# Cached attention with a gated linear unit, one core: keys and probabilities transposed by VectorE in 32x32 blocks instead of by TensorE

## The chip, the core and the metric

The kernel runs on one core of one Trainium2 chip. A core has five engines that run their own instruction streams and wait for each other by semaphores: TensorE (matrix products; PE in the profile, PEld for its weight loads), VectorE (DVE), ScalarE (ACT), GpSimd (POOL) and SyncE (SP), which here only issues transfers. Data lies in HBM, in SBUF (128 partitions) and in PSUM, where TensorE writes its products. Sixteen DMA engines move data between HBM and SBUF. The metric is the device time of one execution in microseconds (us).

## The reference

What is computed, cut to its core (all arrays bf16):

```python
xn = layernorm(x)                                # x: [8, 1, 512]
q = (xn @ wq)                                    # 32 heads of 128
k = k_cache[:, :, 8192 - 2048:, :]               # 8 batches x 8 key heads, last 2048 rows
v = v_cache[:, :, 8192 - 2048:, :]               # each key head serves 4 query heads
scores = einsum("bhqd,bhkd->bhqk", q, k) * 128 ** -0.5
o = einsum("bhqk,bhkd->bhqd", softmax(scores), v)
s = o.reshape(8, 1, 4096) @ wo
g = (sigmoid(xn @ w_gate) * (xn @ w_up)) @ w_down   # inner width 1792
out = x + s * silu(g)
```

The window of both caches is 8 x 8 x 2048 x 128 numbers each, 33.6 MB, and the weights are 14 MB.

## The kernel before

**Slots and transfers.** Nine SBUF slots of 2 MB (`slots`) hold weights and tiles of the caches. A list `todo`, filled at lines 171 to 192, fixes the order of all transfers: w_gate, w_up, w_down with some small side loads, wq, then K and V tiles, with V three tiles behind K, then wo in four pieces. `pump` issues the next transfer on SyncE's queue as soon as a slot is empty, and `free` gives a slot back at the place in the program where its last reader stands. The side loads (`want_side`, line 122) carry the 384 rows of w_down that the 128-partition load `want_down` leaves out; each touches 3, 5 or 9 partitions.

**A cache tile** (`want_cache`) holds half of the key heads of one batch: four heads `l`, 32 partitions `p` each, with partition 4p + l, and 64 rows `c` of 128 numbers in each partition. So one batch has two K tiles and two V tiles, i = 0 and 1.

**The head of the program** normalises x, computes the gated unit (L278, L294, L366), the queries (`q_ps`, L352: 32 matmuls, four at a time on four column strips of the array), turns them by TensorE (L380) and lays them into `qm_sb`, where each head's four columns stand in a band of zeros, so that a shifted view puts them into any group of four rows.

**The batch loop** (from line 647) is an order of work written out by hand. Each batch has 16 steps. Each step transposes 8 blocks of a K tile on TensorE (`k_transposes`, L456), which VectorE copies from PSUM to `kT_sb` (L461); tasks hang on the steps:

- `scores` (L474): every second step, four matmuls of 512 columns side by side on four strips of 32 columns. A row of `s_ps` is one query head and one of four parts j of its keys.
- `row_max` (L487, L494): the maximum of each of the 128 rows, then four exponentials, each over 32 rows x 512, into `p_buf`.
- `stat_rows`, `factor`, `spread` (L506 to L556): the four parts of a head have maxima of their own; these steps bring them together and make one factor for each row, on one partition.
- `p_transposes` (L563, L568): 16 transposes of the probabilities by TensorE, copied by VectorE to `pT_sb`. Their operand is read in steps of 32 bytes.
- `value` (L584): the products with V, two batches later. Up to batch 4 these are pairs of matmuls of 512 columns on two strips, from batch 5 on fours of 256 columns on four strips.
- `combine`, `normalise`, `turn` (L604, L614, L623, L632, L639): scale the output, pick the right blocks, and lay them as a column into `oP_sb`.

A K slot is freed behind its last transposes, a V slot behind its last value matmul. Behind the loop follow the last two batches' rest, and the product with wo (L706, 128 matmuls of 128 columns), the gate and the residual (L717, L719) and four small output transfers (L721).

Of the kernel before, what the change touches and what calls it, by code (L numbers as in the profile page):

```python
# [10 lines left out]
def kernel(  # L11
# [24 lines left out]
    G = 4  # L36
# [5 lines left out]
    CH = CU // 2  # L42
    NU = NQ * NJ
    NR = NU * rep
# [19 lines left out]
        tc.tile_pool(name="ps_t", bufs=4, space=bass.MemoryType.PSUM)  # L64
# [5 lines left out]
        tc.tile_pool(name="ps_o", bufs=1, space=bass.MemoryType.PSUM)  # L70
# [40 lines left out]
    LOW, SF = (5, 5, 3, 3), 15  # L111
    MID, SM = 9, 4
    SP = 4 * max(LOW)
    M_AT = 32
    MP = 4 * MID
    MT = 11
    m0 = MT * P
    m1 = m0 + SF * sum(LOW)
    assert m1 + SM * MP == F
    side = {}  # L120

    def want_side(w, q, at, count, rows, base, of):
        def f(tag=None):
            if tag:
                t = slots.tile([P, SF, w.shape[1]], bf16, name="side", tag=tag)
                nc.gpsimd.memzero(t[:M_AT])  # L126
                side["t"] = t
                rows_of[("side", 0)] = (t, tag)
                for r in range(SF):
                    weights[("wd_sb", MT + r)] = t[: M_AT + MP if r < SM else SP, r]  # L130
            q0.dma_start(  # L131
                out=side["t"][at + q : at + q + 4 * (count - 1) + 1 : 4, :rows].rearrange(
                    "p s n -> p (s n)"
                ),
                in_=w[base : base + of * count * rows, :].rearrange(
                    "(p q s) n -> q p (s n)", q=of, s=rows
                )[q % of],
            )

        todo.append((not side, f))  # L140
        side["asked"] = True
# [32 lines left out]
    sides = []  # L174
    for q in range(4):
        sides.append((q, 0, LOW[q], SF, m0 + q // 2 * 2 * LOW[0] * SF, 2))
        sides.append((q, M_AT, MID, SM, m1, 4))
# [13 lines left out]
    for t0, t1 in ((0, 16), (16, 26), (26, 30), (30, RT)):  # L191
# [13 lines left out]
    perm = consts.tile([P, P], bf16, name="perm")  # L205
    nc.gpsimd.tensor_copy(  # L206
        out=perm[:].rearrange("k (l p) -> k l p", l=G),
        in_=ident[:].rearrange("k (p l) -> k l p", l=G),
    )


    x_f = work.tile([B, D], f32, name="x_f")
    nc.vector.tensor_copy(out=x_f[:], in_=x_bf[:])
    stats = work.tile([B, nc.vector.BN_STATS_DIM], f32, name="stats")
    nc.vector.bn_stats(out=stats[:], in_=x_f[:])
# [7 lines left out]
    xn_bf = work.tile([B, D], bf16, name="xn_bf")  # L223
    nc.vector.tensor_scalar(  # L224
        out=xn_bf[:],
        in0=x_f[:],
# [7 lines left out]
    for kt in range(KT):  # L234
        nc.tensor.transpose(  # L235
            out=xnT_ps[:, kt, :],
            in_=xn_bf[:].rearrange("b (p kt) -> b kt p", kt=KT)[:, kt, :],
            identity=ident[:B, :B],
        )
    xnT_sb = work.tile([P, KT, Z], bf16, name="xnT_sb")  # L240
    nc.vector.memzero(xnT_sb[:])
    nc.vector.tensor_copy(out=xnT_sb[:, :, :B], in_=xnT_ps[:])  # L242
# [5 lines left out]
    h_side = work.tile([B, SF, M_AT + MP], bf16, name="h_side")  # L248
# [4 lines left out]
    M0 = Z - rep  # L253
    qm_sb = work.tile([P, B, Hkv, M0 + Z], bf16, name="qm_sb")
    nc.gpsimd.memzero(qm_sb[:])
    p_buf = [work.tile([P, PG, G, CU], bf16, name=f"p_buf{i}") for i in range(2)]
    for t in p_buf:
        nc.gpsimd.memzero(t[:])
# [16 lines left out]
    for k in range(F // FC):  # L275
        g_ps = ps_t.tile([B, FC], f32, name="g_ps", tag="t")
        for kt in range(KT):
            nc.tensor.matmul(  # L278
                g_ps[:],
                lhsT=xnT_sb[:, kt, :B],  # L280
# [9 lines left out]
    h_bf = ktpool.tile([P, CU * P], bf16, name="h_bf", tag="kT")  # L290
    for k in range(F // FC):
        u_ps = ps_t.tile([B, FC], f32, name="u_ps", tag="t")
        for kt in range(KT):
            nc.tensor.matmul(  # L294
                u_ps[:],
                lhsT=xnT_sb[:, kt, :B],
# [12 lines left out]
    for h in range(2):  # L309
# [10 lines left out]
    nc.gpsimd.tensor_copy(  # L320
        out=h_side[:, :SM, M_AT:],
        in_=h_bf[:B, m1:F].rearrange("b (p t) -> b t p", t=SM),
    )
    cuts = [h_bf[:B, :m0].rearrange("b (p t) -> b t p", t=MT)[:, t] for t in range(MT)]
    rows = [P] * MT + [M_AT + MP] * SM + [SP] * (SF - SM)
    cuts += [h_side[:, t, : rows[MT + t]] for t in range(SF)]
# [5 lines left out]
    for k, t0, t1 in ((M_AT + MP, MT, MT + SM), (SP, MT + SM, MT + SF)):  # L332
        nc.scalar.copy(out=hT_sb[:k, t0:t1, :B], in_=hT_ps[:k, t0:t1])
# [13 lines left out]
    q_ps = [ps_t.tile([P, D], f32, name="q_ps", tag="t") for _ in range(2)]  # L347
    for kt in range(KT):
        for e in range(2):
            for g in range(G):  # L350
                c0 = (G * e + g) * D
                nc.tensor.matmul(  # L352
                    q_ps[e][Z * g : Z * (g + 1), :],
                    lhsT=xnT_sb[:, kt, :],
                    rhs=weights[("wq_sb", kt)][:, c0 : c0 + D],
                    start=(kt == 0),
                    stop=(kt == KT - 1),
                    tile_position=(0, Z * g),
                    skip_group_check=True,
# [15 lines left out]
    for e in range(2):  # L375
        q_bf = ktpool.tile([P, D], bf16, name="q_bf", tag="kT")
        nc.scalar.mul(out=q_bf[:], in_=q_ps[e][:], mul=scale)
        qT_ps = ps_t.tile([P, rep, G, Z], bf16, name="qT_ps", tag="t")
        for r in range(rep):
            nc.tensor.transpose(  # L380
                out=qT_ps[:, r].rearrange("p g z -> p (g z)"),
                in_=q_bf[:, r * Dh : (r + 1) * Dh],
                identity=ident[:],
            )
        nc.vector.tensor_copy(  # L385
            out=qm_sb[:, :, G * e : G * (e + 1), M0 : M0 + rep].rearrange(
                "p b g r -> p r g b"
            ),
            in_=qT_ps[:, :, :, :B],
        )  # L390
# [13 lines left out]
    for j in range(NB):  # L404
# [12 lines left out]
    Hh = G * rep  # L417
    turn_rows = consts.tile([P, P], bf16, name="turn_rows")
    nc.gpsimd.tensor_copy(
        out=turn_rows[:].rearrange("k (x l r) -> k x l r", x=NU, l=G),  # L420
        in_=ident[:].rearrange("k (l x r) -> k x l r", x=NU, l=G),
    )
    sel_e = consts.tile([P, 2, Hq], f32, name="sel_e")
    for e in range(2):
        nc.vector.reduce_sum(
            out=sel_e[:, e, :].rearrange("k (i h) -> k i h", i=NQ),
            in_=ident_f[:].rearrange(
                "k (i m e h) -> k e i h m", i=NQ, m=NJ // 2, e=2
            )[:, e],
            axis=AX.X,  # L430
        )

    o_ps = ps_o.tile([P, NJ, Dh], f32, name="o_ps")
    sel_j = ident_f[:].rearrange("k (i j h) -> k j i h", i=NQ, j=NJ)
    m_ps = ps_m.tile([P, 512], f32, name="m_ps", tag="m")
    top_ps = m_ps[0:1, 0:P]
    sum_ps = m_ps[0:1, P : 2 * P]
    fac_ps = m_ps[:, 2 * P : 2 * P + 1]
# [3 lines left out]
    kT = {}  # L442
    s_ps = {}
    pT = {}
    st = {}
    row = {}
    fac = {}

    def k_transposes(b, u, h):
        i, j = u // NJ, u % NJ  # L450
        k_sb = k_tiles[(b, i)][0]
        if h == 0:
            kT[(b, u)] = ktpool.tile([P, CU, P], bf16, name="kT_sb", tag="kT")
        kT_ps = ps_t.tile([P, CH, P], bf16, name="kT_ps", tag="t")
        for c in range(CH):
            nc.tensor.transpose(  # L456
                out=kT_ps[:, c, :],
                in_=k_sb[:, j * CU + h * CH + c, :],
                identity=perm[:],
            )  # L460
        nc.vector.tensor_copy(  # L461
            out=kT[(b, u)][:, h * CH : (h + 1) * CH, :], in_=kT_ps[:]
        )
        if j == NJ - 1 and h == 1:
            free(k_tiles.pop((b, i)))

    def scores(b, u):
        i, j = u // NJ, u % NJ
        if u == 0:
# [285 lines left out]
```

## Time and profile before

| What | Value |
|---|---|
| median of 3 runs | 199.12 us (199.09 to 199.34) |
| the profiled execution | 199.33 us, of which the span from first to last instruction is 197.5 us |
| TensorE busy | 157.4 us (80%), 2112 matmuls |
| TensorE weight loads | 103.1 us (52%) |
| VectorE busy | 125.4 us (63%), 245 instructions |
| ScalarE busy | 40.7 us (21%) |
| GpSimd busy | 11.0 us (6%) |
| moved by DMA | 81.32 MB, mean 412 GB/s |
| clock granted to TensorE | mean 0.965 of full speed |

The page of the profile has six parts: busy time of each engine; the span in 40 equal slices, with a digit for the busy tenths of each engine, of the DMA engines, and of the clock granted to TensorE; the DMA queues; the chain of work that ended last; the costliest groups of instructions by source line; and the transfers. A group's line reads: source line, engine, operation, output and inputs, shape, count, then busy us and mean ns of one, then the idle time of the engine just before them and what ended it. Matmuls are pipelined: the 389 ns of a score matmul run from its start to its last result, while the next group may start sooner. The timeline lists start (us) and length (us) of instructions in order of time.

### The profile page before, as it was taken

The numbers are of one execution on the slowest core, as the hardware profiler recorded it, in microseconds if no ns is written. First come the engines' busy times: TensorE is split into PE (matmuls) and PEld (weight loads), VectorE is DVE, ScalarE is ACT, GpSimd is POOL, SyncE is SP. The second block draws the span as 40 slices with busy tenths as digits, with TensorE's granted clock in tenths as the row PEclk, the third lists the DMA queues.
The fourth block names the chain that finished last, engine by engine and source line by source line (L and its number), as shares of the span: only waits on it lengthen the run. The fifth ranks groups of instructions, "written<-read, shape, count | busy, mean of one in ns | idle before, by whom it ended". The sixth has DMA issues, their size and how long they took to land.

```text
span 197.5 us, 4796 instructions
## 1 busy us (share of the span) xinstructions
PE 157.4 (80%) x2112; PEld 103.1 (52%) x2112; DVE 125.4 (63%) x245; ACT 40.7 (21%) x95; POOL 11.0 (6%) x22
## 2 busy tenths in 40 slices
PE   0089559999788898799979987999799979976733
PEld 0034325776664565466545654566466556655531
DVE  4623106999797696679666965796669658935201
ACT  0522022006306001600160016001600160071000
POOL 8910200000000000000000000000000000000000
PEclk9999859999999999999999999999999999999975
DMA  6999999999999999999999999999999999999980
GB/s 205 424 440 435 431 434 435 425 425 431 423 425 425 438 428 435 431 425 428 422 433 431 435 425 433 428 418 428 428 438 431 428 428 431 428 423 425 428 366 21
DMA packets 6396, 81.32 MB, mean 412 GB/s; under 512 B 812, under 2 KB 820, under 8 KB 1624
## 3 DMA queue, kind: packets, MB, share of 16 engines
q1 hardware_dynamic: 6328, 81.01, 96.6%
q8 instruction: 16, 0.26, 0.5%
q10 hardware_dynamic: 48, 0.01, 0.0%
q14 instruction: 4, 0.03, 0.0%
HBM read 81.01 MB, written 0.01 MB: 410 GB/s over the span
## 4 chain that ended last, share of the span: by engine, by line
DMA 73%; PE 22%; POOL 3%; SPq 0%; issue 0%; DVE 0%; POOLq 0%
DMA v_sb<-in_A_v_cache_dram 46%; DMA wo_sb<-in_A_wo_dram 14%; PE kT_ps L456 11%; DMA wq_sb<-in_A_wq_dram 7%; DMA k_sb<-in_A_k_cache_dram 6%; PE o_ps L584 4%; PE s_ps L474 3%; POOL side L126 2%; PE m_ps L614 1%; PE fin_ps L706 1%; PE pT_ps L563 1%; SPq L131 0%; POOL perm L206 0%; POOL hT_sb L245 0%; DVE prod L717 0%
## 5 line engine op out<-in xcount | busy, mean ns | idle before, releaser
L461 DVE COPY kT_sb<-kT_ps 128x1024 bf16<-128x1024 bf16 x128 | 84.2, 683 | 28.9 <-PE kT_ps L456 25.0
L456 PE MATMUL kT_ps<-perm,k_sb 128*128 128x128 bf16 x1024 | 72.6, 220 | 3.7 <-DMA k_sb<-in_A_k_cache_dram 3.7
L456 PEld LDWEIGHTS <-k_sb 128*128 128x128 bf16 x1024 | 58.8, 98 | 26.1 <-issue 16.8
L584 PE MATMUL o_ps<-v_sb,pT_sb 128*32 128x256 bf16 (+1 forms) x352 | 36.5, 327 | 9.0 <-DMA v_sb<-in_A_v_cache_dram 7.6
L474 PE MATMUL s_ps<-kT_sb,qm_sb 128*32 128x512 bf16 x256 | 25.6, 389 | 1.3 <-DVE kT_sb L461 1.1
L494 ACT ACTIVATE p_buf<-s_ps,st 32x512 bf16<-32x512 f32 x32 | 21.7, 679 | 15.4 <-DVE st L487 15.1
L584 PEld LDWEIGHTS <-pT_sb 128*32 128x32 bf16 (+1 forms) x352 | 12.3, 101 | 21.7 <-issue 19.7
L604 ACT ACTIVATE o_sb<-o_ps,fac 128x512 f32<-128x512 f32 (+1 forms) x8 | 4.9, 608 | 60.9 <-PE o_ps L584 60.9
L568 DVE COPY pT_sb<-pT_ps 128x1024 bf16<-128x1024 bf16 x16 | 10.8, 676 | 1.8 <-PE pT_ps L563 1.8
L474 PEld LDWEIGHTS <-qm_sb 128*32 128x32 bf16 x256 | 7.0, 93 | 8.0 <-issue 1.3
L563 PE MATMUL pT_ps<-turn_rows,p_buf 128*128 128x128 bf16 x128 | 10.7, 227 | 0.0
L563 PEld LDWEIGHTS <-p_buf 128*128 128x128 bf16 x128 | 9.4, 149 | 0.2 <-issue 0.2
L521 ACT ACTIVATE w_row<-w 1x128 f32<-1x128 f32 x8 | 2.5, 309 | 30.6 <-DVE w L514 30.6
L235 PE MATMUL xnT_ps<-ident,xn_bf 8*128 8x8 bf16 x4 | 0.3, 176 | 10.6 <-DVE xn_bf L224 10.6
L385 DVE COPY qm_sb<-qT_ps 128x128 bf16<-128x128 bf16 x2 | 1.4, 881 | 8.7 <-PE qT_ps L380 8.7
L301 DVE TENSOR_TENSOR h_bf<-sig,u_ps 8x448 bf16<-8x448 f32 x4 | 2.4, 608 | 6.6 <-PE u_ps L294 6.1
L278 PE MATMUL g_ps<-wg_sb,xnT_sb 128*8 128x448 bf16 x16 | 5.7, 544 | 0.3 <-DVE xnT_sb L242 0.3
L494 ACT ACTIVATION_READ_ACCUMULATOR p_buf<-s_ps,st 32x1 f32 x32 | 5.9, 184 | 0.0
L706 PE MATMUL fin_ps<-wo_sb,oP_sb 128*32 128x128 bf16 x128 | 3.3, 263 | 3.1 <-DMA wo_sb<-in_A_wo_dram 3.1
L487 DVE TENSOR_REDUCE st<-s_ps 128x1 f32<-128x512 f32 x8 | 5.4, 681 | 0.5 <-PE s_ps L474 0.5
L235 PEld LDWEIGHTS <-xn_bf 8*128 8x128 bf16 x4 | 0.2, 117 | 10.6 <-DVE xn_bf L224 10.6
L352 PE MATMUL q_ps<-wq_sb,xnT_sb 128*32 128x512 bf16 x32 | 3.1, 526 | 3.2 <-DMA wq_sb<-in_A_wq_dram 3.2
(88 smaller groups left out, 92.0 us busy)
## 6 DMA issues: line engine op xcount, KB each, us to landing
k_sb<-in_A_k_cache_dram SPq DMA_DIRECT2D x16, 2048.0 KB
v_sb<-in_A_v_cache_dram SPq DMA_DIRECT2D x16, 2048.0 KB
wq_sb<-in_A_wq_dram SPq DMA_DIRECT2D x2, 2048.0 KB
wo_sb<-in_A_wo_dram SPq DMA_DIRECT2D x1, 2048.0 KB
wg_sb<-in_B_w_gate_dram SPq DMA_DIRECT2D x2, 896.0 KB
wu_sb<-in_B_w_up_dram SPq DMA_DIRECT2D x2, 896.0 KB
wd_sb<-in_B_w_down_dram SPq DMA_DIRECT2D x1, 1408.0 KB
wo_sb<-in_A_wo_dram SPq DMA_DIRECT2D x1, 1280.0 KB
```

Of the source, the lines that this page charges most:

```text
L126: nc.gpsimd.memzero(t[:M_AT])
L278: nc.tensor.matmul(g_ps[:], lhsT=xnT_sb[:, kt, :B], rhs=weights[("wg_sb", kt)][:, k * FC : (k + 1) * FC], start=(kt == 0), stop=(kt == KT ...
L456: nc.tensor.transpose(out=kT_ps[:, c, :], in_=k_sb[:, j * CU + h * CH + c, :], identity=perm[:],)
L461: nc.vector.tensor_copy(out=kT[(b, u)][:, h * CH : (h + 1) * CH, :], in_=kT_ps[:])
L474: nc.tensor.matmul(s_ps[b][NR * l : NR * (l + 1), :], lhsT=qm_sb[:, b, i * G + l, o : o + Z], rhs=t[:, :, PG * l : PG * (l + 1)], start=(u ...
L487: nc.vector.tensor_reduce(out=st[b][:], in_=s_ps[b][:], axis=AX.X, op=ALU.max, negate=True)
L494: nc.scalar.activation(out=p_buf[b % 2][rows, :, l, :], in_=s[rows, :].rearrange("k (c p) -> k p c", p=PG), func=AF.Exp, bias=st[b][rows, ...
L563: nc.tensor.transpose(out=pT_ps[:, c, :], in_=p_buf[b % 2][:, :, :, h * CH + c].rearrange("k p l -> k (p l)"), identity=turn_rows[:],)
L568: nc.vector.tensor_copy(out=pT[b][:, h * CH : (h + 1) * CH, :], in_=pT_ps[:])
L584: nc.tensor.matmul(o_ps[r] if b < WIDE else o_ps[r, 0:2], lhsT=pT[b][:, c, r], rhs=x, start=(c == 0), stop=(c == CU - 1), tile_position=(0 ...
L604: nc.scalar.activation(out=o[:, :n], in_=o_ps[:, :n], func=AF.Copy, scale=fac.pop(b)[:])
L706: nc.tensor.matmul(fin_ps[Z * j : Z * (j + 1), :], lhsT=oP_sb[:, t, :], rhs=weights[("wo_sb", t)][:, j * P : (j + 1) * P], start=(t == 0), ...
```

## The change

The keys are no longer transposed by TensorE. `k_turn` takes a quarter of a K tile, reads each pair of bf16 numbers as one 4-byte number, and has VectorE transpose all 32x32 blocks of these in place; no PSUM and no copy are involved. After that a partition holds one pair of the 128 numbers, for the keys of one group of 32 partitions (a group `a` holds eight p of all four heads). So `scores` multiplies with a stationary operand of full width, `q_wide`, in which the query stands once for each of the four groups of partitions, in blocks, with zeros around; two halves j of the pairs, four heads l and two members e of the pair make 16 matmuls of 512 columns for a tile, and the moving operand takes every eighth number (16 bytes apart). A row of `s_ps` is now (group a, tile i, head l, query r), a column (c, h).

One maximum per query head replaces the maxima of four parts: `row_max` reduces the rows and turns the 128 values into one row; `head_max` takes the maximum over the four groups and brings it back to all rows by a matmul with one column. `exps` then makes four exponentials over all 128 rows, one for each l, with a scale of 1 or 0 and a bias of minus the maximum or -1000, so that rows of another head give 0. `p_turn` transposes the probabilities as pairs in 32x32 blocks by VectorE. `factor` adds up the sums by one matmul.

`widen` copies the queries of a batch into one of two `q_wide` buffers on GpSimd, four copies per batch; a batch has eight steps instead of 16. The query matmuls use the full array. K slots are freed behind the scores. The values are pairs of matmuls on two strips in all batches, four rows c at a time, and have two PSUM buffers. The side loads carry 128 rows of w_down (8 rows per partition, in two halves each), and the 128-partition load 13 rows per partition instead of 11. The first 16 of 32 products with wo are done as 16 matmuls of 512 columns, copied by ScalarE and folded in by fp32 matmuls (`fold`).

The diff, cut to its core:

```diff
-    LOW, SF = (5, 5, 3, 3), 15
-    MID, SM = 9, 4
+    LOW, SF, SH = (5, 5, 3, 3), 8, 4
     SP = 4 * max(LOW)
-    M_AT = 32
-    MP = 4 * MID
-    MT = 11
+    MT = 13
     m0 = MT * P
...
-                    q_ps[e][Z * g : Z * (g + 1), :],
-                    lhsT=xnT_sb[:, kt, :],
...
+                    q_ps[i][:],
+                    lhsT=xnT_sb[:, kt, X0 - B * l : X0 - B * l + P],
...
+        nc.vector.transpose(
+            out=qT[:, i].rearrange("p r j z e -> p (r j z e)").bitcast(f32),
+            in_=q_bf[:].bitcast(f32),
+        )
+
+    def widen(b):
+        t = q_wide[b % 2]
+        for a in range(PG // B):
+            g = slice(Z * a, Z * (a + 1))
+            nc.gpsimd.tensor_copy(
+                out=t[g, : NW * P].rearrange(
+                    "p (i x e c) -> p i x e c", i=NQ, x=2 * G, e=2
+                )[:, :, :, :, M0 + Z * a : M0 + Z * a + rep],
+                in_=qT[g].rearrange("p i r j (l b) e -> p i (j l) b e r", b=B)[
+                    :, :, :, b
+                ],
+            )
 
...
-        kT_ps = ps_t.tile([P, CH, P], bf16, name="kT_ps", tag="t")
-        for c in range(CH):
-            nc.tensor.transpose(
-                out=kT_ps[:, c, :],
-                in_=k_sb[:, j * CU + h * CH + c, :],
-                identity=perm[:],
-            )
-        nc.vector.tensor_copy(
-            out=kT[(b, u)][:, h * CH : (h + 1) * CH, :], in_=kT_ps[:]
-        )
...
+    def k_turn(b, s):
+        i, j = s // NJ, s % NJ
+        x = (
+            k_tiles[(b, i)][0][:, j * CU : (j + 1) * CU, :]
+            .rearrange("p c d -> p (c d)")
+            .bitcast(f32)
+        )
+        nc.vector.transpose(out=x, in_=x)
+
+    def scores(b, i):
+        if i == 0:
+            s_ps[b] = ps_s.tile([P, CT, 2 * NA], f32, name="s_ps", tag="s")
+        k = k_tiles[(b, i)][0][:].rearrange(
+            "p c (j h l e) -> p j l e c h", j=2, h=2 * NA, l=G
+        )
+        for n in range(NW // NQ):
+            j, l, e = n // (2 * G), n // 2 % G, n % 2
+            o = (i * (NW // NQ) + n) * P + M0 - NL * i - rep * l
             nc.tensor.matmul(
-                s_ps[b][NR * l : NR * (l + 1), :],
-                lhsT=qm_sb[:, b, i * G + l, o : o + Z],
-                rhs=t[:, :, PG * l : PG * (l + 1)],
-                start=(u == 0),
-                stop=(u == NU - 1),
-                tile_position=(0, NR * l),
-                skip_group_check=True,
-            )
-
+                s_ps[b][:],
+                lhsT=q_wide[b % 2][:, o : o + P],
+                rhs=k[:, j, l, e],
+                start=(i == 0 and n == 0),
+                stop=(i == NQ - 1 and n == NW // NQ - 1),
+            )
+        free(k_tiles.pop((b, i)))
 
...
+        nc.tensor.transpose(out=top_ps, in_=st.pop(b)[:], identity=ident_f[:])
+
+    def head_max(b):
+        low = small.tile([1, NA, NQ * NL], f32, name="low")
+        nc.vector.tensor_reduce(
...
+        nc.tensor.matmul(
+            all_ps,
+            lhsT=low[:].rearrange("o a x -> o (a x)"),
...
+        bias = small.tile([P, G], f32, name="bias")
+        nc.vector.scalar_tensor_tensor(
+            out=bias[:],
+            in0=mask[:],
+            scalar=all_ps,
+            in1=away[:],
+            op0=ALU.mult,
+            op1=ALU.add,
+        )
+        row[b] = bias
+
+    def exps(b):
+        bias = row.pop(b)
         s = s_ps.pop(b)
+        p_buf[b] = ppool.tile([P, CT // 2, 2 * NA, G, 2], bf16, name="p_buf")
+        sums[b] = small.tile([P, G], f32, name="sums")
         for l in range(G):
-            rows = slice(NR * l, NR * (l + 1))
             nc.scalar.activation(
-                out=p_buf[b % 2][rows, :, l, :],
-                in_=s[rows, :].rearrange("k (c p) -> k p c", p=PG),
+                out=p_buf[b][:, :, :, l, :],
+                in_=s[:].rearrange("k (c e) h -> k c h e", e=2),
                 func=AF.Exp,
-                bias=st[b][rows, :],
-                accum_out=sums[rows, :],
-            )
...
+                bias=bias[:, l : l + 1],
+                scale=mask[:, l : l + 1],
+                accum_out=sums[b][:, l : l + 1],
+            )
+
+    def p_turn(b):
+        pT[b] = ppool.tile([P, NQ, CT // 2, NL, 2], bf16, name="pT_sb")
+        nc.vector.transpose(
+            out=pT[b][:]
+            .rearrange("p i c x e -> p (i c x e)")
+            .bitcast(f32)
+            .rearrange("p (i c x) -> p c i x", i=NQ, x=NL),
+            in_=p_buf.pop(b)[:].rearrange("k c p l e -> k (c p l e)").bitcast(f32),
+        )
 
...
+        nc.tensor.matmul(
+            sum_ps,
+            lhsT=spread_f[:].rearrange("k i m x e -> k (i m x e)"),
+            rhs=sums.pop(b)[:],
+            start=True,
+            stop=True,
         )
         fac[b] = small.tile([P, 1], f32, name="fac")
-        nc.vector.tensor_copy(out=fac[b][:], in_=fac_ps)
-
...
+        nc.vector.reduce_sum(out=fac[b][:], in_=sum_ps, axis=AX.X)
+        nc.vector.reciprocal(out=fac[b][:], in_=fac[b][:])
+
...
+    NS = NQ * NJ
     for b in range(B):
...
+        tasks = {s: [] for s in range(NS)}
         if b >= 1:
+            tasks[0].append(lambda: scores(b - 1, 1))
+            tasks[1].append(lambda: row_max(b - 1))
+            tasks[2].append(lambda: head_max(b - 1))
+            tasks[2].append(lambda: exps(b - 1))
+            tasks[6].append(lambda: p_turn(b - 1))
+            tasks[6].append(lambda: factor(b - 1))
+        tasks[0].append(lambda: widen(b))
+        tasks[4].append(lambda: scores(b, 0))
+        if b >= 2:
+            for s in range(NJ, NS):
+                n = (s - NJ) * NN // NJ
+                tasks[s].append(lambda n=n: values(b - 2, n, n + NN // NJ))
         if b >= 3:
...
+            tasks[0].append(lambda: combine(b - 3))
+            tasks[3].append(lambda: normalise(b - 3))
+            tasks[5].append(lambda: turn(b - 3))
+        for s in range(NS):
+            k_turn(b, s)
             for f in tasks[s]:
                 f()
 
...
+    RG = 16
+    f_ps = ps_t.tile([P, D], f32, name="f_ps", tag="t")
+    for t in range(RG):
+        g = slice(Z * (t % G), Z * (t % G + 1))
+        nc.tensor.matmul(
+            f_ps[g, :],
+            lhsT=oP_sb[:, t, :],
+            rhs=weights[("wo_sb", t)],
+            start=(t < G),
+            stop=(t >= RG - G),
+            tile_position=(0, g.start),
+            skip_group_check=True,
+        )
+    f_sb = ktpool.tile([P, D], f32, name="f_sb", tag="kT")
+    nc.scalar.copy(out=f_sb[:], in_=f_ps[:])
+    for t in range(RG, RT):
+        if t == 26:
+            fold(fin_ps, f_sb, False, False)
```

## The prediction

> **What bounds the kernel now.** I read the 40 slices first, then the queues, then the chain that ended last, then the groups, and last the timeline and the windows of the end.
>
> ```profile
> DMA  6999999999999999999999999999999999999980
> ...
> q1 hardware_dynamic: 6328, 81.01, 96.6%
> q8 instruction: 16, 0.26, 0.5%
> ...
> DMA 73%; PE 22%; POOL 3%; SPq 0%; issue 0%; DVE 0%; POOLq 0%
> ```
>
> The DMA engines are full from the first slice to the last but one. Queue q1 takes 96.6% of 197.5 us on 16 engines, 190.8 us of each, and its packets run from 1.8 to 193.4 us: no gap is left. q8 fetches instructions, 16 packets of 16 KB at 929 ns (the packets of the trace), 0.93 us of each engine. The 22% of TensorE in the chain are stretches in which the transfers ran on anyway. So the time is a start of 1.8 us, 191.6 us of full DMA engines, and a tail of 4.1 us behind the last packet. The changed kernel moves the same cache and weights; it is faster only through fewer fetches or a shorter tail, and slower only if computation falls so far behind that the transfers wait for slots, or that the last batch ends after the last weights are there.
>
> How much room there is: a 2 MB tile takes 4.9 us (k15 ends 162.95 us, k14 153.20, with one V tile between them), a batch of two K and two V tiles 19.6 us. Issues of cache tiles lie 18 us or more ahead of their first packets from the second batch on.
>
> ```profile
> L461 DVE COPY kT_sb<-kT_ps 128x1024 bf16<-128x1024 bf16 x128 | 84.2, 683 | 28.9 <-PE kT_ps L456 25.0
> L456 PE MATMUL kT_ps<-perm,k_sb 128*128 128x128 bf16 x1024 | 72.6, 220 | 3.7 <-DMA k_sb<-in_A_k_cache_dram 3.7
> L456 PEld LDWEIGHTS <-k_sb 128*128 128x128 bf16 x1024 | 58.8, 98 | 26.1 <-issue 16.8
> L474 PE MATMUL s_ps<-kT_sb,qm_sb 128*32 128x512 bf16 x256 | 25.6, 389 | 1.3 <-DVE kT_sb L461 1.1
> L563 PEld LDWEIGHTS <-p_buf 128*128 128x128 bf16 x128 | 9.4, 149 | 0.2 <-issue 0.2
> L487 DVE TENSOR_REDUCE st<-s_ps 128x1 f32<-128x512 f32 x8 | 5.4, 681 | 0.5 <-PE s_ps L474 0.5
> ```
>
> These are the groups that the change replaces (L456, L461, L563) or prices.
>
> **Part 1: instructions removed.** 1,024 transposes of keys and 128 of probabilities go, with their weight loads. The built program has 1,474 rows on TensorE, 4,091 before, so 16 fetches become about 5.8: 10 × 0.929 / 16 = 0.6 us less per engine if spread evenly. The side loads of w_down shrink with it (384 rows to 128; the other 256 join the 128-partition load), same bytes. Even so engines may end unevenly: the last packets ended between 192.6 and 193.4 us. I take **-0.6** (0 to -0.9).
>
> **Part 2: turning the keys.** 64 transposes of 128x1024 pairs and 8 of probabilities replace 144 copies of 0.68 us. The trace has no VectorE transpose. Nearest below is the copy, 683 ns. A reduction of 512 elements took 681 ns, one of 128 (L264) 274 ns: 1.06 ns an element, so 1024 at one per cycle take 0.274 + 0.95 = 1.22 us. The upper end is L267, which reads the same 128 elements in steps of 64 bytes, in 356 ns: at its 2.1 ns an element, 2.1 us. Each block reads whole runs, so I take 1.22. VectorE then has 9 × 1.22 + 2 × 0.68 + about 1.0 = 13.3 us in 19.6: not a bound. At 2.1 us it would have 21.3, 1.7 × 8 = 14 us too much.
>
> [...]
>
> **Part 3: scores.** 32 matmuls of 512 columns a batch, as before, but over the full array, not four side by side. Alone one streams at 213 ns: pairs of 512-column o_ps matmuls follow each other in 0.21 to 0.24 us in the trace, and fours of 256 columns in 0.10 to 0.11. So 0.33 us for four becomes 0.85. New is the moving operand: its columns lie 16 bytes apart. No matmul of before does that. From below: 213 ns. The nearest row on the same engine are weight loads:
>
> ```profile
> 166.26 0.45 PEld L456 LDWEIGHTS <-k_sb 128*128 128x128 bf16 x8 [0.21 <-issue]
> 166.67 0.58 PEld L563 LDWEIGHTS <-p_buf 128*128 128x128 bf16 x8
> ```
>
> Columns of k_sb lie side by side, those of p_buf 32 bytes apart. Start to start the median is 56 and 63 ns: 63 / 128 × 512 = 252 ns. From above: VectorE's L267 against L264 pays 0.64 ns an element more, 213 + 328 = 541 ns. I take 250 ns, since it is the engine's own read path, and 213 to 541 for the range.
>
> [...]
>
> **Part 4: the order, which is now a chain.** On both engines each step waits for the one in front, once per batch, counted from the last turn of one batch to that of the next: scores of the second half 16 × 0.25 + 0.2 (389 ns from start to end, less 213) = 4.2; row maximum 0.68; a turn 1.22 (it covers the transpose of the maxima); the maximum per head, 512 elements read, 0.68; matmul and bias 0.4; a turn 1.22; scores of the first half 4.0; eight pairs of value matmuls at 0.213, 1.7; turn(b-3) and its copy 0.5; a turn, the probabilities and the last turn 3.66; the factor 0.3. Sum **18.6 us**, 17.4 with 213 ns, against 19.6 us of data. The exponentials (4 × 0.86 on ScalarE, as now) fit beside it. A K slot comes free after its scores, some 10.5 us behind its landing; before it was 7.4 (k15 there at 164.5, its slot used by SP at 171.9): 3 us out of 18 of lead. So the chain stays under the transfers by 1.0 to 2.2 us a batch and I charge nothing; cover gone, each microsecond over counts 7 times.
>
> The head: 32 query matmuls of the full array, 6.8 us against 3.1, and POOL's four copies per batch (0.3 to 0.45 us like L312) put the first turn at about 35.5 us instead of 33.2. The first slot so freed carries a load whose first packet is at 74 us. Nothing.
>
> **Part 5: the tail.**
>
> ```profile
> 188.81 1.08 PE L706 MATMUL fin_ps<-wo_sb,oP_sb 128*32 128x128 bf16 x64 [1.12 <-DMA wo_sb<-in_A_wo_dram]
> ...
> 191.86 2.28 PE L706 MATMUL fin_ps<-wo_sb,oP_sb 128*32 128x128 bf16 x64 [1.97 <-DMA wo_sb<-in_A_wo_dram]
> ```
>
> The first 64 become 16 wide ones and a ScalarE copy (0.6), done by 191. Into the 2.28 us behind 191.86 come four fp32 folds, eight rows; the like at L337 took 0.43 us at full clock, so up to 0.86 at the half clock here, less the 0.39 us that TensorE idles there between landings: 0.04 to 0.47. I take **+0.2**.
>
> **Sum.** -0.6 + 0.2 = -0.4: span 197.5 to 197.1, the profiled execution 199.33 to 198.9, and, as that one stands 0.2 over the median, **198.7 us** on 199.12. Its own range is 197.9 to 199.4.
>
> **Rivals.**
>
> *The clock is halved and the chain overshoots (slower).* The place is the 4.2 us between the two halves of the scores, where TensorE has only the small matmuls of the maxima and of normalise, about 1.1 us.
>
> ```profile
> 183.44:186.85 3.41, 2.55 (x39) 2.10 (x38) 0.46 (x2) 0.47 (x1) 0.00 (x0) 1.00 0.98 422
> 186.85:190.27 3.42, 1.53 (x68) 1.27 (x68) 0.59 (x2) 0.00 (x0) 0.00 (x0) 1.00 0.95 402
> 190.27:193.70 3.43, 1.84 (x56) 1.48 (x56) 0.00 (x0) 0.00 (x0) 0.00 (x0) 0.50 0.60 240
> ```
>
> Columns: busy time of PE, PEld, DVE, ACT, POOL, the clock, DMA. After a window with TensorE busy 75% the clock stayed 1.00, after 45% it was 0.50; windows of 57% elsewhere kept it. A half-clock window of 3.41 us costs 1.7 us of a burst. One a batch: 17.4 + 1.7 = 19.1, still hidden, or at 250 ns 20.3, 0.7 × 7 = 5 us. Two: 22, 17 us. So 200 to 216, about 204; it decides from 1.0 to 2.2 us of loss a batch. For it: the gap is in the order of the code; against: one lost window is absorbed at 213 ns. [...]
>
> *Strided scores at half rate or worse (slower).* At 430 to 541 ns the chain grows by 32 × 0.18 to 0.29: 24.4 to 27.9 us, 4.8 to 8.3 over, seven times: 232 to 257.
>
> *Nothing gained.* The fetches lie on engines that are not last, the fold costs 0.5: 199.0 to 199.4.
>
> **Chances.** Forecast 0.45 (a part of it gains under 0.2%, about what a measurement of this kernel can tell from no change), nothing gained 0.2, half clock 0.22, strided scores or slow turns 0.13. Faster by over 0.2% 0.42, within 0.2% 0.23, slower 0.35. The range 197.9 to 209 takes in the first three but the rival's far end.
>
> **What would show it.** L465 at 1.2 us; the new scores spaced 0.21 to 0.25 us; clock 1.00 from 30 to 190 us; SP waiting, yet DMA nines in every slice; five to six packets on q8; the last o_sb before 188 us. Wrong if 0.50 stands in the middle windows, if scores lie 0.4 us apart, or if DMA slices fall under nine.

## The result, and the profile after

The changed kernel takes **374.16 us** (median of 4 runs, 372.93 to 375.95), the kernel before 199.13 beside it: 1.879 times as long (95% interval 1.871 to 1.888). The prediction was 198.7 us with a range to 209. Here and below medians hold all runs of a kernel, ratios leave disturbed ones out.

The page of the changed kernel, the slices, the two queues and the chain by engine and by line:

```profile
PEclk9999555555555855565555655565555655585698
DMA  8999999945141954169505762277505960320000
...
q1 hardware_dynamic: 6288, 81.01, 53.3%
q8 instruction: 6, 0.10, 0.1%
...
PE 81%; DVE 8%; DMA 6%; issue 2%; POOL 1%; SPq 0%; ACT 0%; ACTq 0%; DVEq 0%
PE s_ps L476 59%; PE o_ps L568 14%; DMA wq_sb<-in_A_wq_dram 4%; DVE k_sb L465 3%; PE m_ps L596 3%; DMA wu_sb<-in_B_w_up_dram 3%; DVE st L487 1%; PE m_ps L506 1%; DVE low L497 1%; PE q_ps L337 1%; POOL q_wide L371 1%; PE m_ps L550 1%; DVE pT_sb L541 1%; DVE oP_sb L621 1%; PE f_ps L679 0%
```

The same 81.01 MB move, but from the ninth slice on the DMA digits fall: transfers wait for slots. 81% of the chain is TensorE now, and most of that is one line, the scores. The groups and, from the timeline of TensorE, the scores of one half:

```profile
L476 PE MATMUL s_ps<-k_sb,q_wide 128*128 128x512 bf16 x256 | 222.5, 1036 | 11.9 <-POOL q_wide L371 6.0
L465 DVE STREAM_TRANSPOSE k_sb<-k_sb 128x1024 f32<-128x1024 f32 x64 | 75.5, 1218 | 0.0
...
L568 PE MATMUL o_ps<-v_sb,pT_sb 128*64 128x512 bf16 x256 | 53.5, 560 | 0.6 <-DVE fac L558 0.6
```

```profile
161.92 3.62 PE L568 MATMUL o_ps<-v_sb,pT_sb 128*64 128x512 bf16 x16
165.48 13.91 PE L476 MATMUL s_ps<-k_sb,q_wide 128*128 128x512 bf16 x16
```

Sixteen scores take 13.9 us: start to start they lie 838 to 861 ns apart in the trace, where I had taken 250. They do so at both clocks: 20 such distances stand in stretches with a granted clock of 1.00, 213 in stretches of 0.50. The o_ps pairs do follow the clock, 213 to 216 ns a pair at 1.00 and 426 at 0.50. So a score's time does not follow TensorE's clock; whether the step of its operand sets its time is what experiments 1 and 2 test. And the clock is halved though TensorE is busy all through these stretches (windows: busy PE, PEld, DVE, ACT, POOL, clock, DMA share, GB/s):

```profile
149.30:152.70 3.40, 3.40 (x5) 0.48 (x4) 0.00 (x0) 0.00 (x0) 0.00 (x0) 0.50 0.00 0
152.70:156.10 3.40, 3.40 (x5) 0.49 (x4) 0.00 (x0) 0.00 (x0) 0.00 (x0) 0.50 0.00 0
```

**Where the 176.7 us between the spans (197.45 and 374.15) lie.** The row maximum (L487) stands once in each batch. In before the first starts at 45.4 us, the last at 173.6; in after at 66.4 and 343.5. So 21.0 us come up to the first, 148.9 in the seven batches between (41.1 us each in the middle, 19.5 before), and 6.8 behind the last. By spacing: 256 scores × (0.86 − 0.213) = 166 us. Values at half clock come to it, up to 128 pairs × 0.214 = 27 us, and what the transfers would have taken anyway goes off; how these two divide is not worked out here.

### The profile page after: what moved, and what is told of

It reads as the page before. It is cut to its first block, busy times and chain, and to the rows that moved or that the text cites. A ratio compares the mean times of both kernels' runs of the same rounds, so it can differ in the third digit from the quotient of the medians.

```text
span 374.1 us, 2156 instructions
## 1 busy us (share of the span) xinstructions
PE 321.6 (86%) x833; PEld 81.7 (22%) x834; DVE 113.3 (30%) x151; ACT 40.5 (11%) x87; POOL 21.3 (6%) x53
## 3 DMA queue, kind: packets, MB, share of 16 engines
q1 hardware_dynamic: 6288, 81.01, 53.3%
HBM read 81.01 MB, written 0.01 MB: 217 GB/s over the span
## 4 chain that ended last, share of the span: by engine, by line
PE 81%; DVE 8%; DMA 6%; issue 2%; POOL 1%; SPq 0%; ACT 0%; ACTq 0%; DVEq 0%
PE s_ps L476 59%; PE o_ps L568 14%; DMA wq_sb<-in_A_wq_dram 4%; DVE k_sb L465 3%; PE m_ps L596 3%; DMA wu_sb<-in_B_w_up_dram 3%; DVE st L487 1%; PE m_ps L506 1%; DVE low L497 1%; PE q_ps L337 1%; POOL q_wide L371 1%; PE m_ps L550 1%; DVE pT_sb L541 1%; DVE oP_sb L621 1%; PE f_ps L679 0%
## 5 line engine op out<-in xcount | busy, mean ns | idle before, releaser
L476 PE MATMUL s_ps<-k_sb,q_wide 128*128 128x512 bf16 x256 | 222.5, 1036 | 11.9 <-POOL q_wide L371 6.0
L465 DVE STREAM_TRANSPOSE k_sb<-k_sb 128x1024 f32<-128x1024 f32 x64 | 75.5, 1218 | 0.0
L476 PEld LDWEIGHTS <-q_wide 128*128 128x128 bf16 x256 | 31.2, 126 | 182.2 <-issue 176.0
L568 PE MATMUL o_ps<-v_sb,pT_sb 128*64 128x512 bf16 x256 | 53.5, 560 | 0.6 <-DVE fac L558 0.6
L530 ACT ACTIVATE p_buf<-s_ps,bias,mask 128x512 bf16<-128x512 f32 x32 | 25.1, 805 | 167.1 <-DVE bias L514 167.1
L487 DVE TENSOR_REDUCE st<-s_ps 128x1 f32<-128x512 f32 x8 | 5.5, 691 | 107.7 <-PE s_ps L476 107.7
L568 PEld LDWEIGHTS <-pT_sb 128*64 128x64 bf16 x256 | 19.8, 152 | 33.2 <-issue 28.3
L371 POOL COPY q_wide<-qT 32x128 bf16<-32x128 bf16 x32 | 12.8, 400 | 216.4 <-PE s_ps L476 214.9
L596 PE MATMUL m_ps<-ident_f,o_sb 128*128 128x32 f32 x56 | 12.4, 383 | 2.5 <-DVE bias L514 2.5
L596 PEld LDWEIGHTS m_ps<-ident_f,o_sb 128*128 128x128 f32 x56 | 11.7, 308 | 3.2 <-issue 3.2
L541 DVE STREAM_TRANSPOSE pT_sb<-p_buf 128x1024 f32<-128x1024 f32 x8 | 9.6, 1203 | 0.0
```

Source lines behind the costliest of these rows:

```text
L371: nc.gpsimd.tensor_copy(out=t[g, : NW * P].rearrange("p (i x e c) -> p i x e c", i=NQ, x=2 * G, e=2)[:, :, :, :, M0 + Z * a : M0 + Z * a + ...
L465: nc.vector.transpose(out=x, in_=x)
L476: nc.tensor.matmul(s_ps[b][:], lhsT=q_wide[b % 2][:, o : o + P], rhs=k[:, j, l, e], start=(i == 0 and n == 0), stop=(i == NQ - 1 and n == ...
L487: nc.vector.tensor_reduce(out=st[b][:], in_=s_ps[b][:].rearrange("k c h -> k (c h)"), axis=AX.X, op=ALU.max,)
L530: nc.scalar.activation(out=p_buf[b][:, :, :, l, :], in_=s[:].rearrange("k (c e) h -> k c h e", e=2), func=AF.Exp, bias=bias[:, l : l + 1], ...
L541: nc.vector.transpose(out=pT[b][:] .rearrange("p i c x e -> p (i c x e)") .bitcast(f32) .rearrange("p (i c x) -> p c i x", i=NQ, x=NL), in ...
```

## The experiments

Theory A: the 16-byte step of the scores' moving columns is the whole loss. Rivals: B, the full-width form or the turn in place is slow; later C, half clock, and D, the length of the last batch's chain, for what A leaves.

**1. The step taken away** (scores from the wrong keys, all else as in the change).

```diff
-            "p c (j h l e) -> p j l e c h", j=2, h=2 * NA, l=G
+            "p (j l e c) (h d) -> p j l e c (h d)", j=2, l=G, e=2, h=1
...
```

> The changed kernel, but each score matmul reads 512 columns that lie side by side (the wrong numbers for the scores: the pairs of four rows c instead of one member of every pair). Nothing else is touched. Theory A (steps): a moving operand read in steps of 16 bytes streams at 860 ns per 512 columns at either clock, and that alone takes the time. Then the spacing of the scores falls from 860 to 213 to 240 ns, and the time from 374 to what the prediction reckoned: 198.7 us, or 200 to 216 if the half clock stays in the gaps of TensorE (theory C). Theory B (width): the scores are slow because each needs a stationary operand of full width and a tile that VectorE has just rewritten in place. Then the spacing stays at 860 ns and the time at 374.

**203.35 us** (ratio 1.020, 1.019 to 1.022). Its page, slices and groups:

```profile
PEclk9999999699795899589957996998599859999999
DMA  6999999999999999999999999999999999999920
...
L465 DVE STREAM_TRANSPOSE k_sb<-k_sb 128x1024 f32<-128x1024 f32 x64 | 76.4, 1223 | 22.1 <-DMA k_sb<-in_A_k_cache_dram 22.1
L476 PE MATMUL s_ps<-k_sb,q_wide 128*128 128x512 bf16 x248 | 73.3, 457 | 4.3 <-POOL q_wide L371 3.7
```

Scores fall to 216 ns at clock 1.00 and 427 at 0.50, the DMA nines are back, and 171 of 175 us are gone. A holds, B falls. About 4 us over before are left.

**2. The price of a step by itself** (no attention, no gated unit: runs of 24 matmuls of 512 columns out of loaded keys, columns so many bytes apart).

> Only matmuls of 128x128 by 512 columns, a new stationary operand for each, 24 of each kind: columns side by side, in steps of 4, 8, 16, 32 and 64 bytes, and two side by side out of each 8 bytes; the attention and the gated unit are left out. Theory A: 213 ns side by side at full clock, 860 ns at 16 bytes at full and at half clock, 4 and 8 bytes between these (213 if a line of 16 bytes counts, 430 at 8 bytes if two hits are needed), 32 and 64 bytes as 16. Theory B: 213 ns in all. If strided reading itself brings the half clock, the granted clock falls during the 16-byte stretch (21 us of TensorE without a gap).

```profile
21.42 5.34 PE L33 MATMUL s_ps<-k,w 128*128 128x512 bf16 x23
26.60 5.58 PE L36 MATMUL s_ps<-k,w 128*128 128x512 bf16 x24
...
33.80 9.21 PE L39 MATMUL s_ps<-k,w 128*128 128x512 bf16 x20 [0.27 <-issue]
42.84 21.78 PE L42 MATMUL s_ps<-k,w 128*128 128x512 bf16 x24
...
76.78 11.00 PE L51 MATMUL s_ps<-k,w 128*128 128x512 bf16 x24
88.52 21.29 PE L45 MATMUL s_ps<-k,w 128*128 128x512 bf16 x23 [0.74 <-issue]
109.63 20.75 PE L48 MATMUL s_ps<-k,w 128*128 128x512 bf16 x24
```

Start to start: side by side (L33) 216 ns, 4-byte steps (L36) 226, 8 (L39) 451, 16 (L42) 900, 32 (L45) 918, 64 (L48) 857; two columns side by side out of every 16 bytes (L51; the kernel takes two of each eight numbers, so it is not 8 bytes, as the expectation says) 451. The price doubles from 4 to 8 and from 8 to 16 bytes and then stays. One count fits all these rows: how many stretches of 16 bytes the 512 columns touch. At 16 bytes they touch 512, 900 / 512 = 1.76 ns each; at 8 bytes and in L51 256, 451 / 256 = 1.76; at 4 bytes 128, 226 / 128 = 1.77; at 32 and 64 bytes again 512, 1.79 and 1.67. L51 tells this from a price of the step: two columns of it lie side by side, and it still costs what 8-byte steps do. A window of the 4-byte and one of the 16-byte stretch show the clock again (columns as above, without ACT):

```profile
26.70:30.10 3.40, 3.40 (x17) 1.43 (x15) 0.00 (x0) 0.00 (x0) 1.00 0.02 5
46.90:50.30 3.40, 3.40 (x5) 0.50 (x4) 0.00 (x0) 0.00 (x0) 0.50 0.00 0
```

Both are busy for the whole window; the stepped one is granted half. The stretches at 451 ns, 9.2 and 11.0 us of busy TensorE, kept 1.00.

**3. A short step for the whole computation, by the turn.** The turn writes each head's eight columns together, so the scores read 4-byte steps.

```diff
-        nc.vector.transpose(out=x, in_=x)
+        nc.vector.transpose(
+            out=x.rearrange("p (b l h) -> p b h l", l=G, h=2 * NA), in_=x
+        )
...
-            "p c (j h l e) -> p j l e c h", j=2, h=2 * NA, l=G
+            "p c (j l h e) -> p j l e c h", j=2, h=2 * NA, l=G
```

> The changed kernel, whole, but VectorE writes each transposed block in another order (head before key), so that a score matmul reads its columns in steps of 4 bytes, runs of 8, instead of 16 bytes. Theory A, if the price is one 16-byte line per column: four columns now share a line, spacing 213 to 250 ns, time as in the kernel with runs, 198 to 216. Theory A, if any step over 2 bytes has a price: 430 ns (about 232 us in all) or 860 (374). Theory B: 860 ns and 374 us. The turn writes in steps of 32 bytes: 1.22 us if that is free; about 2.1 us if it costs VectorE as the stepped read at L267 did, and then 21 us of VectorE for 19.6 us of data in a batch, 10 to 16 us more in all.

**237.71 us** (1.194, 1.190 to 1.198). This is more than the 208 to 232 us that the expectation adds up to. The scores are cured, 217 ns at clock 1.00 and 427 at 0.50, with four columns to 16 bytes as in L36, but the step has moved to VectorE:

```profile
L465 DVE STREAM_TRANSPOSE k_sb<-k_sb 128x1024 f32<-128x1024 f32 x64 | 121.5, 1973 | 0.0
```

Writing in 32-byte steps costs 1.97 us a turn instead of 1.22, 8 × 0.75 = 6.0 us a batch; row maxima lie 24 us apart.

**4. The kernel before with the same step** (its four-strip scores read keys 16 bytes apart, the wrong ones).

```diff
-                rhs=t[:, :, PG * l : PG * (l + 1)],
+                rhs=t[:].rearrange("p c (x s) -> p s c x", s=8)[:, 2 * l : 2 * l + 2],
...
```

> The kernel before, but each of its four score matmuls that run side by side reads its 512 columns in steps of 16 bytes from the same transposed tile (the wrong keys for the scores). Theory A with four strips that read at once: a four takes 0.86 us instead of 0.21 of streaming, 64 fours, 42 us more of TensorE in a kernel where it sits idle for 40: 199 to 212 us. Theory A with strips that share one reader: 3.4 us a four, 3.2 x 64 = 205 us more, 380 to 400. Theory B: no change, 199.1.

**221.48 us** (one run, before 199.28), over the 199 to 212 expected. The four strips still run side by side and pay the step together: from the start of a four to the next instruction 1.00 us pass, 0.33 in before. So a four pays 0.67 us, about what one full-width matmul pays (0.86 − 0.21). Before issues 64 such fours, the change 256 matmuls of the full array; the full width therefore pays the step four times as often.

**5. A short step by the loads.** K tiles loaded in another row order by four loads of 32 partitions, plain turns, 4-byte steps; and the same with extra matmuls (see 7).

> The changed kernel with the keys of each partition loaded in another order (four loads of 32 partitions for each K tile instead of one of 128, same bytes), so that the plain turn leaves the columns of the scores' moving operand 4 bytes apart instead of 16. All of the reference is computed. Theory A (the step of the moving columns alone made the kernel slow): scores spaced 213 to 230 ns where the granted clock is 1.00 and about 427 at 0.50, turns 1.22 us, DMA nines again to the end, and a time like that of the side-by-side run, 203.3 us (202 to 205), the rest over 199.2 being the half clock. Rival: the four smaller loads have a price of their own, DMA under nines and 206 us or more.

> The run with the other load order, with 20 extra matmuls of 512 columns a batch (identity times identity, into a tile that nobody reads) where TensorE waits for the maxima and the turns. All of the reference is computed. Theory C (the 4 us left over 199.2 are the half clock that TensorE gets for the gaps of the chain): granted clock 1.00 in the middle stretches, scores and values spaced 213 ns, the last o_sb near 188 us instead of 194, 198.3 to 199.5 us. Rival D (the chain is too long whatever the clock: turns, row maximum, waits): clock 1.00 and still 202 us or more. Rival E: the extra matmuls stand in the way of the chain's own: later still than the run without them, 205 us or more.

**512.14 and 511.66 us** (2.571 and 2.569): my expectation of 203 missed by far. Scores and turns were as hoped, but the loads were not. The slices of the first:

```profile
DMA  8922254362726345272726345272725439996420
GB/s 347 413 109 108 108 163 136 136 167 105 193 106 178 122 153 150 112 186 108 196 109 177 123 152 150 106 195 109 196 103 168 134 135 225 289 240 171 153 106 24
```

In stretches with keys alone 108 GB/s, a quarter of 430: the packets of the trace keep their 0.61 us (all 40 that began from 120 to 126 us), but four run at a time, not 16. Between them the value tiles arrive, loaded as in the change: 16 packets at a time, but 1.13 to 1.27 us each (from 131 to 137 us, 221 GB/s; the 126 slow packets from 129 to 140 us are about the 128 of one tile). Why these are slow here stays open.

**6. One head to each group of 32 partitions**, so that the turn itself leaves 32 keys of one head in 4-byte steps, with one exponential a batch instead of four. First with one load a tile, then with four (one a head), then with these four on two queues; each with and without extra matmuls.

```diff
-                    "l (p c) d -> p l (c d)", c=CT
+                    "l (p c) d -> l p (c d)", c=CT
...
+            for l in range(G):
+                q0.dma_start(
+                    out=t[Z * l : Z * (l + 1)].rearrange("p c d -> p (c d)"),
...
-                q0.dma_start(
+                (q0, q1)[l // 2].dma_start(
```

> All of the reference is computed. Same loads of 128 partitions and 16 KB runs as the changed kernel, but a partition group holds one head's keys instead of a row of all four heads', so that the plain turn leaves 32 keys of one head side by side in pairs: the scores' moving columns lie 4 bytes apart. Still 32 score matmuls of 512 columns and 64 turns a batch group of two K tiles as before (256 and 64 in all); one exponential of 512 columns a batch instead of four, and the probabilities turned in four pieces of 32 partitions. Theory A (the step alone made the kernel slow): scores spaced 213 to 230 ns at clock 1.00, turns 1.22 us, DMA nines to the end. Theory D (what the run with side-by-side columns had over 199.2 is the length of the last batch's chain, not the clock): the three exponentials of 0.81 us that go shorten it by 2.4 us, 199 to 201 us even at half clock in parts. Theory C (the clock alone): 203 us as there.

> The run with one head to a partition group, with 20 extra matmuls of 512 columns a batch (12 in the last) where TensorE waits. All of the reference is computed. If chain and clock both count: clock 1.00 in the middle and 197.5 to 199.0 us, under the run without them. If only the chain counts: within 0.5 us of it. If the extra matmuls stand in the way: over it by 1 us or more.

> The run with one head to a partition group, each cache tile asked for by four loads of one head each (32 rows of 16 KB into 32 partitions) instead of one load whose outermost dimension is the four heads. All of the reference is computed. If the 690 us of the one-load run came from that outermost dimension of four (packets ran four at a time): 16 packets at a time again, DMA nines, and theory A's and D's numbers: scores 213 to 230 ns at clock 1.00, 199 to 201 us. If the order of heads in the partitions itself is slow (32 partitions at a time): again near 690 us. Theory C (the clock alone): 203 us.

> The same with 20 extra matmuls of 512 columns a batch (12 in the last) where TensorE waits. All of the reference is computed. If chain and clock both count: clock 1.00 in the middle, 197.5 to 199.0 us, under the run without them. If only the chain counts: within 0.5 us of it. If the extra matmuls stand in the way: 1 us or more over it.

> The run with one head to a partition group and four loads a tile, two of them asked for by SP and two by ScalarE, so that two groups of 32 partitions are written at a time. All of the reference is computed. If a group of 32 partitions takes at most 213 GB/s: two at a time take 426, packets at 0.6 us again, DMA bound as before, and 198.5 to 202 us by theories A and D. If the loads are slow for another reason (many small loads): near 359 us.

> The same with the extra matmuls (20 a batch, 12 in the last). All of the reference is computed. If the transfers are back at 426 GB/s: 197.5 to 199.5 us, clock 1.00 in the middle; under the two-queue run without them by what the half clock costs there. If near 359: within 1 us of that run.

One load: **689.92 and 692.35 us** where 199 to 201 was expected, 109 GB/s, four packets at a time again. Four loads: **358.62 and 358.82** (1.800 and 1.796). Their slices:

```profile
DMA  8999999999999999999999999999999999999993
GB/s 309 442 384 208 213 220 211 213 222 208 214 220 209 215 211 220 207 215 219 213 215 208 224 213 209 220 209 216 213 217 213 211 213 215 216 213 219 215 320 145
```

Nines, yet 213 GB/s: 16 packets at a time, each taking 1.23 us instead of 0.61. Two queues: **338.25 and 335.91 us**, not the 198.5 to 202 expected if each group of 32 partitions takes at most 213 GB/s:

```profile
GB/s 230 194 367 268 312 302 224 249 253 251 249 247 224 235 234 242 249 251 253 249 259 249 253 254 226 241 245 243 243 221 232 232 230 226 232 230 231 303 209 1
```

From 62 to 308 us 52% of the packets come from SP's queue and 48% from ScalarE's, 16 run at a time, and yet they take 1.08 us each (median) and together move 241 GB/s. So the loads are slow in two ways: few packets run together, or 16 run and each takes about twice as long. The first goes with the outermost dimension on the side of the caches: it was four where four packets ran at a time (experiment 5's keys and the one load a tile here, 108 and 109 GB/s), and 32 in the changed kernel and with the four loads a tile here, where 16 ran. The second came with loads to 32 adjacent partitions each, 213 GB/s on one queue against 430. Its cause is not shown: two groups of 32 at a time moved 241 and not 426, and the value tiles of experiment 5 go to all 128 partitions and their packets were as slow.

**7. The 4 us that are left.** Extra matmuls keep TensorE busy where the chain waits, in the kernel of experiment 1; then only one exponential in the last batch (three quarters of its probabilities zero), without and with the extra matmuls, of which eight in the last batch are dropped.

```diff
+            tasks[0].append(lambda: fill(3))
...
+            tasks[1].append(lambda: fill(5))
...
+        tasks[3].append(lambda: fill(4))
...
+        tasks[7].append(lambda: fill(8))
...
-        for l in range(G):
+        for l in range(G if b < B - 1 else 1):
```

> The run whose scores read 512 columns side by side (one load of 128 partitions for each K tile, scores from the wrong keys), with the same 20 extra matmuls a batch and nothing else changed. Theory C: 203.3 us become 198.3 to 199.5. Rival D: 202 us or more at a clock of 1.00. Rival E: 205 us or more. Against the run with the other load order it tells whether that order costs anything: within 0.5 us of each other if not.

> The run whose scores read 512 columns side by side (scores from the wrong keys), with one exponential instead of four in the last batch alone (three quarters of its probabilities are left zero). Theory D (the 4 us over 199.2 are the last batch's chain, which runs on after the transfers end): 3 x 0.81 = 2.4 us less, 200.5 to 201.3 us. Theory C (the half clock in the middle): unchanged, 203.3.

> The same with the extra matmuls (20 a batch, 12 in the last, none between the last value matmuls and the last scores). If chain and clock both count: the run with all extra matmuls (203.0) less 2.4 for the exponentials and less 8 x 0.213 = 1.7 for the eight left out, 198.9 us (198.3 to 199.6). If only the chain counts: as the run without extra matmuls, 200.5 to 201.3. If neither: 203.

**203.04 us** (1.016, 1.011 to 1.021), **202.57** (1.013, 1.012 to 1.014), **200.40** (1.004, 1.002 to 1.005). By the ratios these lie 3.1, 2.6 and 0.7 us over before, experiment 1 4.0. Extra matmuls alone bring the clock of the profiled execution from 0.888 to 0.965, but the gain of 0.9 us is not clear, since the intervals overlap; eight of them stand in front of the last scores and may take back up to 1.7. A shorter last batch alone gains 1.4 us of the 2.4 expected, so neither C nor D by itself gives its number. Both together, without those eight, gain 3.3. The place is the last batch. In before and in the kernel of experiment 1, ScalarE's last row before the end:

```profile
185.96 0.47 ACT L604 ACTIVATE o_sb<-o_ps,fac 128x256 f32<-128x256 f32 x1 [7.12 <-PE o_ps L584]
```

```profile
191.51 0.69 ACT L588 ACTIVATE o_sb<-o_ps,fac 128x512 f32<-128x512 f32 x1 [9.33 <-PE o_ps L568]
```

The transfers of experiment 1 end at 192.1 us, 1.3 earlier than before's 193.4, but the last o_sb ends at 192.2 instead of 186.4: the output weights wait for it. With both cures it ends at 190.1, in a span of 198.0. In this profile of experiment 1 (201.90 us) the clock is 1.00 from 165.5 to 199.6 us, so what is lost there is the chain's. From the start of the last row maximum to the end of the last o_sb 17.3 us pass, 12.8 in before, and most of that stands in the values of the last batch:

```profile
179.17 1.05 PE L584 MATMUL o_ps<-v_sb,pT_sb 128*32 128x256 bf16 x16 [0.79 <-DVE pT_sb L568]
182.39 1.05 PE L584 MATMUL o_ps<-v_sb,pT_sb 128*32 128x256 bf16 x16
183.95 1.92 PE L584 MATMUL o_ps<-v_sb,pT_sb 128*32 128x256 bf16 x32
```

```profile
182.96 1.91 PE L568 MATMUL o_ps<-v_sb,pT_sb 128*64 128x512 bf16 x8 [0.61 <-DVE fac L558]
185.81 1.91 PE L568 MATMUL o_ps<-v_sb,pT_sb 128*64 128x512 bf16 x8
187.78 3.64 PE L568 MATMUL o_ps<-v_sb,pT_sb 128*64 128x512 bf16 x16
```

Before does them in fours on four strips, 4.0 us. The change does the last batch's 32 one after the other, first those of tile 0 and then those of tile 1, 7.5 us, where the batches in the loop do them in pairs. No run here pairs them. How the 4 us of the median divide between clock and chain stays open, and no version of the whole computation beat the kernel before.

## Why the prediction was wrong

- **What bounds now, and the room**: right. With the step gone the batches lie 19.4 us apart, at the pace of the transfers.
- **Part 1, fetches**: right in kind, 6 packets on q8. The last packet of the loads stands 1.3 us earlier in experiment 1, beyond my 0 to 0.9; where the rest comes from is not shown.
- **Part 2, turns**: right, 1.218 us against 1.22. That a turn goes at the 1.06 ns an element of the two reductions was my estimate; the trace of before has no turn. The upper end was misread: L267's 82 ns over 128 elements make 1.06 + 0.64 = 1.7 ns an element, not 2.1, so 1.9 us; the stepped turn of experiment 3 took 1.97.
- **Part 3, scores: the step that failed.** I took 250 ns, upper end 541; it is 860. I called the strided weight loads "the engine's own read path" and carried their 63 ns per 128 columns over. For the moving operand 32-byte steps cost 918 ns per 512 columns, 230 per 128: a weight load shows next to nothing of that price, so its row was no bound for it. Nor was VectorE's 0.64 ns an element: TensorE pays 1.26 a column. Two columns to 16 bytes still cost 451 ns (8-byte steps); with four it is 226 (4-byte steps).
- **Part 4, the chain**: its other terms were good. 18.6 + 32 × (0.86 − 0.25) = 38.1 us, and the eight pairs of values in it add 1.7 at half clock: 39.8, against 41.1 measured. Of the rest 1.0 lies between the row maximum and the next scores, 5.2 us where its terms make 4.2.
- **Part 5, the tail**: wrong. "All done by 191" needs the last o_sb before 188; it came at 192.2 even with columns side by side. The last batch's values, one after the other, had no term.
- **The half-clock rival**: its 204 us is close to the 203.35 of experiment 1 by chance. No loss was multiplied by seven: in the middle the half clock stayed hidden (batches 19.4 us apart, DMA nines), and what shows lies in the last batch. Nor does a window's busy share decide the clock, as I read it from 75% and 45%: in before the window from 19.60 us is busy 68% and 0.50 follows, that from 9.37 us 57% and 1.00 follows, and the change is granted 0.50 at 100%.
- **The stepped-scores rival**: the right mechanism with too low an end, 541 ns, and so 257 us (its 430, half rate, was my estimate too: no run shows it at 16-byte steps, 8-byte steps took 451); together with slow turns I gave it 0.13.
- **The forecast's own range**, 197.9 to 199.4, is not what its terms add up to: -0.9 to 0 and 0.04 to 0.47 make 198.3 to 199.6.

## What to carry to other kernels

A layout that saves instructions is priced by the innermost step of every operand that reads it, in bytes: for TensorE's moving operand, count the stretches of 16 bytes that the columns touch (1.7 to 1.8 ns each in experiment 2). Where no row shows that operand with that step, the range stays open upwards, and a row of another operand of the same engine doesn't close it. Moving the step to the writer or to the loads only moved the price here (turns of 1.97 us, loads at 108 to 241 GB/s): ask for each of the three what it pays. Look at whether a matmul's spacing follows the granted clock: where it did not here (838 to 861 ns at 1.00 and at 0.50), the step of its columns had set it.

## What the runs showed of the hardware

- From start to start a matmul of 512 columns takes 216, 226, 451, 900 ns with moving columns 2, 4, 8, 16 bytes apart, no more beyond (918 at 32, 857 at 64), and 451 with two side by side out of every 16 bytes: 1.7 to 1.8 ns for each 16 bytes touched once the columns are stepped. At 16 bytes the time is the same at clock 1.00 and 0.50 (838 to 861 ns in the changed kernel).
- Weight loads pay next to none of this: 63 ns for 128 columns 32 bytes apart, 56 side by side.
- TensorE with matmuls 838 to 900 ns apart is granted 0.50 in most stretches (213 of 233 such distances in the changed kernel) though its busy share is 100%; at 451 ns it kept 1.00.
- Four strips side by side pay the 16-byte step once: a four takes 1.00 us instead of 0.33.
- VectorE's turn of 128x1024 4-byte numbers takes 1.22 us, and 1.97 when it writes in 32-byte steps.
- 16 KB packets: 0.61 us each, 16 at a time, in before and in the changed kernel; four at a time, 108 and 109 GB/s, in experiment 5's keys and the one-load run of experiment 6, whose source had an outermost dimension of four; 16 at a time at 1.23 us each with loads to 32 adjacent partitions, at 1.08 with two such groups from two queues.
